# Batch 0's score steps in another order, and corner blocks cleared one group later

## The chip, the cores and the metric

One core of one Trainium2 chip. The metric is the device time of the whole program in microseconds (us), as the median of several runs. Each run has beside it the mean clock that TensorE was granted, as a share of full speed (1.0).

## The reference, cut to what matters

Eight batches of block-causal attention over 576 tokens (8 heads of 64, blocks of 64) are joined to 4608 tokens of 512 channels, which pass through an RMS norm and a gated feed-forward network (FFN).

```python
scores = scale * np.matmul(q, k.transpose(0, 1, 3, 2))      # 8 x 8 heads, 576 x 576
mask = block_i >= block_j                                   # blocks of 64
attn = np.exp(scores - max);  attn = attn / (sum + 1e-9)    # cut
x = (attn @ v), heads joined                                # 4608 x 512
rms = np.sqrt(np.mean(x * x, axis=-1, keepdims=True) + 1e-6)
xn = x / rms * rms_g
out = (silu(xn @ w_gate) * (xn @ w_val)) @ w_out            # 512 -> 1536 -> 512
```

## The kernel before

Heads go in pairs (b, t). `scores` makes a piece of S^T on TensorE, and ScalarE writes its exponential, unmasked, into `PT`. In each diagonal 128x128 tile one 64x64 corner lies outside the mask; VectorE sets it to zero (the "corner memset"). `values` multiplies by V: the P V product. `group` is one step of the FFN for 512 tokens (8 or 16 products on TensorE, `th` on ScalarE, then `gs` and `HT` on VectorE), and groups are laid between the attention steps so that TensorE always has something to do. The "scales" (`norm_scale`) multiply O^T, the output of P V, by the RMS factor; the result is `XT`, the input of the groups. The "ends" (`scores_ends`) are small 64x64 score blocks that are left over at the ends of the tokens.

```python
def clear(age=0):                                  # corner memsets, in VectorE's queue
    while corners and corners[0][0] <= gone - age:
        nc.vector.memset(corners.pop(0)[1], 0.0)

def scores_exp(pt, sp, step):
    nc.scalar.activation(out=pt[...], in_=sp[...], func=AF.Exp, scale=SCALE)
    for c, q0, w, o in parts:
        if c and q0 == c * P:                      # a diagonal tile: note its corner
            corners.append((gone, pt[BLK:P, :, lo + o:lo + o + BLK]))

def group(n=1):
    for _ in range(n):
        clear()                                    # every corner noted so far, AHEAD of gs and HT
        ...                                        # (cut) one FFN group: ffn_up or ffn_down
        gone += 1                                  # gone counts groups

def evacuate(outs, early=False):                   # behind a P V product
    ...                                            # O^T copy (VectorE if early, else ScalarE),
                                                   # then its square SQ on VectorE
```

The main sequence of batch 0 (cut; `FIRST` and `SECOND` are the two halves of the queries):

```python
scores(0, 0, "a"); transpose_pair(0, 1); scores(0, 0, "b"); fill(2)     # fill: zero matmuls
...                                                                     # (cut)
scores(0, 3, "a")
clear()                                             # all four pairs' corners at once
values(0, 0, FIRST, early=True)
values(0, 1, FIRST, early=True)
scores_ends(0)
...                                                 # (cut)
outs = values_mm(0, 0, SECOND, early=True)
...
group()
evacuate([head_product(0, ...)], True)
values(0, 2, SECOND, early=True)
values(0, 3, SECOND, early=True)
group()
```

The softmax here doesn't subtract the row's maximum and nothing guards it: scores larger than these inputs give would overflow.

## Time and profile before

| | before |
|---|---|
| time, median of 3 runs | 410.11 us (409.37 to 410.35) |
| span of the profiled run | 407.4 us |
| TensorE busy | 385.6 us, 95% |
| mean granted clock | 0.995 |

Two rows of the page that cut the span into 40 slices: TensorE's busy share in tenths, and the granted clock in tenths.

```profile
PE   7789799999999999999999999999999999999995
...
PEclk9989999999999999999999999999999999999999
```

The single 8 in the clock row is the third slice, 20 to 30 us: there lies the one stretch at half clock, 3.4 us long, and it costs the 0.005 by which the mean stays under 1. TensorE's longest waits, each as "engine, what it wanted to write, its line, the engine and tile that released it: us in total, how often, the longest".

```profile
PE fps L375 <- DVE w L367: 2.8, 6, 1.0
PE fps L451 <- DVE XT L420: 2.3, 9, 0.4
PE sps L237 <- DVE KT L206: 1.4, 3, 0.6
```

No P V product (L284) waits for the corner memset (L223).

### The profile page before, as it was taken

What the parts mean: (1) busy time and instruction counts of PE and PEld (TensorE: products, weight loads), DVE (VectorE), ACT (ScalarE), POOL (GpSimd) and SP (SyncE); (2) the same over time, 40 slices, a digit from 0 to 9 for tenths busy, and PEclk for the clock granted to TensorE, in tenths of its full rate; (3) what the DMA queues carried; (4) which work ended last, traced back from release to release, by engine and by line L of the source; (5) the groups of instructions that cost most, each with busy time, mean ns of one, the idle gap of its engine ahead of it and who ended that gap; (6) DMA issues with size and microseconds to landing.
All of it is one profiled execution on the core that took longest, in us unless ns stands there. A gap on an engine that the chain in (4) does not pass through costs nothing.

```text
span 407.4 us, 7780 instructions
## 1 busy us (share of the span) xinstructions
PE 385.6 (95%) x3048; PEld 183.7 (45%) x3087; DVE 251.3 (62%) x620; ACT 197.1 (48%) x283; POOL 129.0 (32%) x181
## 2 busy tenths in 40 slices
PE   7789799999999999999999999999999999999995
PEld 3468566444434444444444444444434434444442
DVE  5676876577777745376727764666457777555430
ACT  3825572466547753465546654565445213332321
POOL 8827773845028062670068004200110010100000
PEclk9989999999999999999999999999999999999999
DMA  8999999999919689999079915500020000010112
GB/s 108 171 202 186 188 140 154 174 137 172 111 53 127 69 78 129 139 139 116 2 108 138 139 19 77 79 0 2 28 78 2 0 27 26 15 38 27 51 52 78
DMA packets 139765, 36.43 MB, mean 89 GB/s; under 512 B 129233, under 2 KB 136913, under 8 KB 139729
## 3 DMA queue, kind: packets, MB, share of 16 engines
q0 software_dynamic: 108448, 26.75, 67.1%
q1 hardware_dynamic: 30752, 9.18, 15.4%
q8 instruction: 24, 0.39, 0.4%
q14 instruction: 13, 0.10, 0.1%
q10 hardware_dynamic: 528, 0.00, 0.1%
HBM read 38.80 MB, written 9.44 MB: 118 GB/s over the span
## 4 chain that ended last, share of the span: by engine, by line
PE 82%; DVE 10%; ACT 3%; issue 2%; DMA 1%; POOL 1%; DVEq 0%; ACTq 0%; POOLq 0%
PE fps L451 41%; PE fps L467 22%; PE sps L237 6%; PE sps L284 4%; PE fps L324 3%; DVE HT L459 2%; DVE XT L420 2%; DVE gs L457 2%; PE fps L284 2%; PE fps L427 1%; ACT th L455 1%; DMA nt<-in_k_dram 1%; PE fps L375 1%; ACT PT L245 1%; PE fps L199 1%
## 5 line engine op out<-in xcount | busy, mean ns | idle before, releaser
L451 PE MATMUL fps<-XT,WG 128*128 128x512 bf16 (+1 forms) x460 | 111.8, 358 | 3.6 <-DVE XT L420 2.3
L245 ACT ACTIVATE PT<-sps 128x1024 bf16<-128x1024 f32 (+1 forms) x96 | 93.8, 989 | 41.3 <-PE sps L237 40.8
L451 PE MATMUL fps<-XT,WV 128*128 128x512 bf16 (+1 forms) x479 | 110.9, 358 | 0.1
L457 DVE SCALAR_TENSOR_TENSOR gs<-th,fps 128x512 bf16<-128x512 f32 x108 | 74.2, 687 | 58.1 <-ACT th L455 56.9
L455 ACT ACTIVATE th<-fps 128x512 f32<-128x512 f32 x108 | 64.7, 599 | 70.7 <-PE fps L451 68.6
L467 PE MATMUL fps<-WO,HT 128*128 128x512 bf16 x416 | 96.4, 379 | 1.2 <-DVE HT L459 0.3
L459 DVE TENSOR_TENSOR HT<-gs,fps 128x512 bf16<-128x512 bf16 x108 | 74.3, 688 | 11.9 <-DVE gs L457 0.9
L451 PEld LDWEIGHTS <-WV 128*128 128x128 bf16 x480 | 46.9, 98 | 48.9 <-issue 3.2
L467 PEld LDWEIGHTS <-HT 128*128 128x128 bf16 x432 | 41.2, 98 | 51.9 <-issue 3.2
L451 PEld LDWEIGHTS <-WG 128*128 128x128 bf16 x480 | 42.3, 98 | 49.0 <-issue 13.3
L470 ACT ACTIVATE osb<-fps 128x512 f32<-128x512 f32 x36 | 21.5, 597 | 81.2 <-PE fps L467 74.2
L478 POOL DMA_DIRECT2D out_dram<-osb x22 | 12.7, 578 | 149.4 <-ACT osb L470 147.7
L123 POOL DMA_DIRECT2D VB<-in_v_dram x48 | 39.6, 845 | 17.3 <-PE sps L284 14.2
L420 DVE SCALAR_TENSOR_TENSOR XT<-OT,gscale,fps 128x64 bf16<-128x64 bf16 (+5 forms) x72 | 30.2, 476 | 21.9 <-PE fps L427 21.9
L237 PE MATMUL sps<-QT,KT 64*128 64x192 bf16 (+5 forms) x280 | 32.9, 310 | 2.6 <-DVE KT L206 1.4
L116 POOL DMA_DIRECT2D nt<-in_q_dram x30 | 26.1, 870 | 7.3 <-DMA VB<-in_v_dram 4.0
L116 POOL DMA_DIRECT2D nt<-in_k_dram x30 | 26.1, 871 | 5.8 <-PE fps L451 1.3
L223 DVE MEMSET PT<- 64x64 uint32 x96 | 9.3, 112 | 23.9 <-ACT PT L245 21.5
L284 PEld LDWEIGHTS <-VB 128*64 128x64 bf16 x344 | 14.7, 113 | 12.7 <-issue 4.4
L481 POOL DMA_DIRECT2D out_dram<-osb x12 | 6.6, 556 | 42.4 <-ACT osb L470 42.4
L237 PEld LDWEIGHTS <-KT 64*128 64x128 bf16 x280 | 9.1, 94 | 23.5 <-issue 18.8
L310 DVE TENSOR_TENSOR SQ<-OT 128x512 bf16<-128x512 bf16 (+1 forms) x44 | 15.7, 373 | 6.1 <-ACT OT L308 5.6
(69 smaller groups left out, 219.8 us busy)
## 6 DMA issues: line engine op xcount, KB each, us to landing
out_dram<-osb POOLq DMA_DIRECT2D x22, 256.0 KB, 2.4
VB<-in_v_dram POOLq DMA_DIRECT2D x32, 128.0 KB, 5.4
nt<-in_q_dram POOLq DMA_DIRECT2D x24, 128.0 KB, 5.5
nt<-in_k_dram POOLq DMA_DIRECT2D x24, 128.0 KB, 5.7
WG<-in_moe_w_gate_dram POOLq DMA_DIRECT2D x4, 384.0 KB, 9.7
WV<-in_moe_w_val_dram POOLq DMA_DIRECT2D x4, 384.0 KB, 10.9
WO<-in_moe_w_out_dram POOLq DMA_DIRECT2D x4, 384.0 KB, 7.7
out_dram<-osb POOLq DMA_DIRECT2D x12, 128.0 KB, 2.6
```

What stands on the lines that cost most here:

```text
L116: nc.gpsimd.dma_start(out=nt[0:rows, 0:512].rearrange("p (h d) -> p h d", h=H), in_=src[b, :, c * P:c * P + rows, :].rearrange("h p d -> p ...
L123: nc.gpsimd.dma_start(out=vb[r:r + n, cc, :].rearrange("p (h d) -> p h d", h=H), in_=v[b, :, tok:tok + n, :].rearrange("h p d -> p h d"))
L237: nc.tensor.matmul(sp[:, a, o:o + w], KT[b][r, t, c * P:(c + 1) * P], QT[b][r, t, q0:q0 + w], start=True, stop=True, skip_group_check=True)
L245: nc.scalar.activation(out=pt[:, :, lo:lo + width], in_=sp[:, :, 0:width], func=AF.Exp, scale=SCALE)
L284: nc.tensor.matmul(ov[a * D:(a + 1) * D, o:o + w], vb[:, c, h * D:(h + 1) * D], rhs, start=(i == 0), stop=(i == len(chunks) - 1), skip_gro ...
L420: nc.vector.scalar_tensor_tensor(out=XT[:, u, y0:y0 + hi - lo], in0=OT[b][:, u, j + lo:j + hi], scalar=gscale[:, u:u + 1], in1=src[:, lo:h ...
L451: nc.tensor.matmul(acc[:, i * w:(i + 1) * w], wt[c][:, p, r * P:(r + 1) * P], XT[:, p, x0:x0 + w], start=(p == 0), stop=(p == HP - 1), ski ...
L455: nc.scalar.activation(out=th, in_=g, func=AF.Tanh, scale=0.5)
L457: nc.vector.scalar_tensor_tensor(out=gs, in0=th, scalar=1.0, in1=g, op0=ALU.add, op1=ALU.mult)
L459: nc.vector.tensor_mul(out=HT[n][:, m:m + k, lo:lo + w], in0=gs.rearrange("p (k w) -> p k w", k=k), in1=u.rearrange("p (k w) -> p k w", k=k))
L467: nc.tensor.matmul(po, HT[n][:, m, i * P:(i + 1) * P], WO[:, m, :], start=(m == 0), stop=(m == NMC - 1))
L470: nc.scalar.mul(out=osb, in_=po, mul=0.5)
```

## The change

Its intent: keep ScalarE fed in batch 0 (its score steps come in another order, P V starts ahead of the last pair's scores), stop VectorE's queue from standing still in front of corner memsets whose exponential has not come yet (they are issued a group later), and put the scales of the second half of batch 0 behind a transpose and one more score step, so that TensorE has work while VectorE catches up. Since a corner can now be still uncleared when its pair's P V product is issued, that product first clears what is left of its own pair. The core of the diff:

```diff
+    def clear_pair(b, t):
+        for c in [c for c in corners if c[1] == (b, t)]:
+            corners.remove(c)
+            nc.vector.memset(c[2], 0.0)
     def values_mm(b, t, part=WHOLE, early=False):
         chunks, j0, width = part
+        clear_pair(b, t)
     def group(n=1):
         for _ in range(n):
-            clear()
+            clear(1)
 # batch 0 (more steps move in the same way; cut)
     scores(0, 3, "a")
-    clear()
-    values(0, 0, FIRST, early=True)
     values(0, 1, FIRST, early=True)        # values(0, 0, FIRST) now stands ahead of scores(0, 3, "a")
 # batch 1
+    transpose_pair(1, 2, on_act="qk")
+    scores(1, 1, 1)
     for u in range(HP):
         norm_scale("b", 0, 256, 320, u)
     mark(S)
-    transpose_pair(1, 2, on_act="k")
-    scores(1, 1, 1)
     group()
 # (cut) the ends of batch 1, scores_ends(1), move up by one group
-    clear()
     values(1, 3, early=True)
 # batch 2, last pair
-            values(2, HP - 1)
+            values(2, HP - 1, early=True)
+            evacuate([head_product(2, ps_f.tile([P, 512], FP32, name="fps"))], True)
```

## The prediction

> **What bounds the kernel now.** I read the page first, then the waits of the engines, then the stretches and the timeline of the first 105 us, because every edited line runs there.
>
> ```profile
> PE 385.6 (95%) x3048; PEld 183.7 (45%) x3087; DVE 251.3 (62%) x620; ACT 197.1 (48%) x283; POOL 129.0 (32%) x181
> PE 82%; DVE 10%; ACT 3%; issue 2%; DMA 1%; POOL 1%; DVEq 0%; ACTq 0%; POOLq 0%
> ```
>
> TensorE is busy 385.6 of 407.4 us and carries 82% of the chain that ended last. So only its idle time, 21.8 us, and any slow clock can be won, and any new idle time on it is lost one for one. The waits name what DVE stands still for:
>
> ```profile
> DVE PT L223 <- ACT PT L245: 21.5, 21, 4.9
> ```
>
> This is the corner memset (96 of them, 112 ns each) waiting in VectorE's queue for the exponential: 21.5 us. It looks like a prize, and "cleared a group later" goes for it. But nobody on TensorE is listed as waiting for these memsets, so in the kernel before it costs nothing.
>
> The stretches of the first 25 us show where TensorE is starved, and what follows:
>
> ```profile
> 18.00:21.30 3.30, 1.48 (x12) 0.73 (x9) 2.23 (x9) 1.81 (x2) 1.89 (x4) 1.00 1.31 203
> 21.30:24.70 3.40, 3.18 (x27) 1.89 (x28) 2.13 (x11) 1.02 (x1) 0.67 (x2) 0.50 1.32 203
> ```
>
> The first number after the length is TensorE's busy time, the third from the end the granted clock: 1.48 us busy in 3.30, then 3.4 us at half clock. Now three places in the timeline where P V products meet VectorE's queue:
>
> ```profile
> 27.85 0.19 DVE L223 MEMSET PT<- 64x64 uint32 x2
> 28.14 0.69 DVE L457 SCALAR_TENSOR_TENSOR gs<-th,fps 128x512 bf16<-128x512 f32 x1
> 28.93 0.69 DVE L459 TENSOR_TENSOR HT<-gs,fps 128x512 bf16<-128x512 bf16 x1
> 29.54 0.42 DVE L306 CAST OT<-fps 128x256 bf16<-128x256 f32 x1
> 29.99 0.29 DVE L310 TENSOR_TENSOR SQ<-OT 128x256 bf16<-128x256 bf16 x1
> ...
> 29.68 1.03 PE L451 MATMUL fps<-XT,WG 128*128 128x256 bf16 x8 [0.16 <-DVE HT L459]
> ```
> ```profile
> 62.47 0.26 DVE L223 MEMSET PT<- 64x64 uint32 x3
> 62.76 0.69 DVE L457 SCALAR_TENSOR_TENSOR gs<-th,fps 128x512 bf16<-128x512 f32 x1
> 62.88 0.79 PE L284 MATMUL fps<-PT,VB 128*64 128x512 bf16 x8
> 63.55 0.69 DVE L459 TENSOR_TENSOR HT<-gs,fps 128x512 bf16<-128x512 bf16 x1
> 63.61 1.05 PE L451 MATMUL fps<-XT,WG 128*128 128x256 bf16 x8
> ```
> ```profile
> 98.90 0.29 DVE L223 MEMSET PT<- 64x64 uint32 x3
> 100.35 0.79 PE L284 MATMUL sps<-PT,VB 128*64 128x512 bf16 x8
> 100.97 0.69 DVE L459 TENSOR_TENSOR HT<-gs,fps 128x512 bf16<-128x512 bf16 x1
> 101.57 0.68 DVE L306 CAST OT<-fps 128x512 bf16<-128x512 f32 x1
> 102.22 0.36 PE L237 MATMUL sps<-QT,KT 64*128 64x448 bf16 x2 [0.63 <-ACT OT L308]
> ```
>
> In each, the memset stands ahead of the gs and HT of the group, so the P V product just behind the group finds its corner already zero.
>
> **What the Trainium skill says.** "PSUM — Partial Sum Buffer", section Engine vs sequencer instructions: the queues of ScalarE and VectorE are strict FIFO. The trace agrees: DVE idles 21.5 us before memsets although later work is queued. "TensorE: Matmul & The Clock Gate", section Part 1: The HAM clock gate: TensorE falls to half clock after an idle window of about 3.4 us, and a free-running window decides. The trace agrees in size: 0.50 for the 3.4 us above. "Perfetto Trace Analysis", section Optimization Strategy: find the gaps of the bounding engine and the semaphore that ends each; I did that on the built order of both programs.
>
> **The change part by part.** The built order shows that all VectorE operations stay the same in number (two copies of Q or K go to ScalarE, one O^T of batch 2 and its head come to VectorE), TensorE gets 3 more filling matmuls (0.23 us each, as eight of that size take 1.83 us in the chain; all in idle time). What moves is what counts.
>
> (a) Batch 0 to its first gated group. P V of pair 0 no longer waits for the exponential of the last pair, so its O^T copy starts at about 14.95 instead of 16.40 us. But each pair's memsets now stand behind the square of the pair before, so DVE and TensorE take turns: 0.46 (copy) + 0.21 (square) + 0.2 (memsets) + 0.3 (last products) = 1.15 us per pair, instead of 0.67. The fourth square ends at about 19.0, where it ended at 19.1. Two fills put the transpose of the sums at about 19.75 (19.49 before). From there to the turned scales it is 4.4 us (19.49 to 23.89 before): about 24.15. Before, the scale products started at 24.66, not 23.9, because TensorE crawled at half clock; with the fills it should be warm. Then one score step is no longer between them and the first group. First group: about 25.9 instead of 26.5. Gain 0.55 us.
>
> (b) The second half of batch 0, pairs 2 and 3. Their last corner's memset now stands behind gs, HT and the head's copy and square. With the gain of (a), HT starts at 28.32, head copy 28.93, square 29.38, memset 29.6 to 29.7 us. Pair 2's product must stop before that corner from 28.3 to 29.75; pair 3's memset waits for pair 2's copy and square (30.0 + 0.46 + 0.21 + 0.1 = 30.8). The next group starts at about 31.0 instead of 29.68: loss 1.3 us net of (a), 1.85 us gross.
>
> (c) The scales of the second half behind a transpose and a score step. Before, from the end of the group at 43.09 to the end of the next at 49.3 us: 6.2 us. After, 1.0 us of transposes and scores fills the first wait, and VectorE has no Q copy there, but gs, HT (0.69 each) and four XT (0.48 start to start) still run one after another, and the group needs all four: about 5.9 us. Gain 0.3 us. The ends moved up save the 0.41 us wait at 53.53 but now wait themselves about 0.5 us for the Q copy behind gs and HT. Net of (c) 0.25 us gained.
>
> (d) P V of pair 2, batch 1: its two last corners are now cleared behind HT and the head (60.59 + 0.46 + 0.21 = 61.26, memset to 61.45), so its last chunks start at 61.42 instead of about 60.7, and the next group at 61.6 instead of 60.98. Loss 0.65 us.
>
> (e) P V of pair 3, batch 1. Counted from the start of the group before it (60.98): gs at +1.78, HT +2.57, memset +3.15, corner products +3.3 to +3.7; before, the next group started at +2.63. Loss 1.05 us.
>
> (f) P V of pair 3, batch 2: its memsets stand behind HT (100.97), pair 2's copy (101.57) and square (102.29): 102.6. The corner products start at about 102.75 and end at 103.2, then head 0.15, two score steps 0.4, next group at 103.8 instead of 102.75. The 0.63 us wait for ScalarE's copy is gone, and is in this difference. Loss 1.05 us.
>
> (g) Batches 3 to 7: a memset a group later still lands before its product, since at least one more group lies between. TensorE's remaining waits there are for w and XT, 0.2 to 0.4 us each, whose chains hold no memset. Zero.
>
> Sum: -0.55 + 1.85 - 0.25 + 0.65 + 1.05 + 1.05 = +3.8 us. To this comes the clock: (b) leaves TensorE idle for some 1.9 of 2.9 us, (c) for most of 3.3 us, and the turn-taking in (a) thins out 14 to 18 us. Half clock for 3.4 us costs up to 1.7 us of bound work. The stretch 41.80 to 45.20 had 1.86 us busy and kept its clock, so not every thin stretch falls. I take 0.5 of one such loss: +0.8 us. 410.1 + 3.8 + 0.8 = 414.7; I say 414.7.
>
> **The rivals.** First: the memset waits matter. 21.5 us of VectorE idle goes away, groups get through VectorE sooner, and TensorE with them. For it: the size, and VectorE is FIFO. Against: no TensorE wait names them, and in the batches that repeat TensorE is busy 98% (48.85 of 50 us from 200 to 250). It would give 405 to 408. Second: the warm clock is the prize. With the half clock gone and the order better for ScalarE, the first 50 us shorten by the idle there (2.3 us in 10 to 20, 1.7 in 20 to 30, 2.2 in 40 to 50 us), with no new stall: 407 to 409. Against: the built order puts memsets behind HT in (b), (d), (e), (f), and TensorE's wait is on exactly these. Third: the new gaps each trip the half clock: three times up to 1.7 us on top of 3.8, 417 to 419. For: the two lines of stretches above; against: 41.80 to 45.20.
>
> **Range and chances.** If the stalls are right and the clock stays, 413.9; if two of them trip it, about 417. If half of the stalls are hidden by something I missed, 412. So 411.3 to 417.8 should hold it 8 times in 10. Faster by over 2% needs under 401.9, more than all idle time of the first 105 us: 0.01. Slower by over 2% needs over 418.3, all clocks tripped: 0.06. The rest, 0.93, is within 2%.
>
> **What would show it.** Right: new lines among TensorE's waits, P V products waiting for the memset, some 1.4, 0.5, 0.7, 1.1 and 2.0 us long, near 28 to 31, 62, 65 and 104 us; the waits of memsets for the exponential nearly gone without gain; clock 1.00 from 21.3 to 24.7 us; stretches after 110 us unchanged but shifted by 4 us. Wrong: if P V never waits for a memset, (b) to (f) fall; if the first group comes later than 26.5 us, (a) falls, most likely by a half clock from 18 us on; if batches 3 to 7 shorten, the first rival is right.

## The result, and the profile after

| | before | after |
|---|---|---|
| time, median of 4 runs each, same chip | 410.21 us (409.37 to 410.35) | 421.33 us (419.27 to 421.49) |
| ratio, with its 95% interval | | 1.0264 (1.0229 to 1.0298): slower |
| span of the profiled run | 407.4 us | 419.7 us |
| mean granted clock, all runs | 0.995 (profiled) | 0.983 to 0.984 |

A ratio here is the mean time of one kernel's runs over that of the other's of the same rounds, so it is not quite the ratio of the medians that are quoted. The change costs 11 us; 4.6 were predicted (414.7 us, with 411.3 to 417.8 as the range).

The page of the changed kernel: TensorE's totals, its busy row and the clock row of 40 slices, and the shares of the chain that ended last.

```profile
PE 395.1 (94%) x3090; PEld 185.3 (44%) x3090; DVE 252.1 (60%) x620; ACT 197.4 (47%) x283; POOL 128.9 (31%) x181
...
PE   8787888999799999999999999999999999999995
...
PEclk9888999999899999999999999999999999999999
...
PE 81%; DVE 12%; ACT 4%; issue 1%; DVEq 0%; ACTq 0%
```

TensorE is busy 9.5 us *longer* than before, for the same work and 3 fills. Some 2 or 3 us of that are records that before's trace lacks (3048 matmuls against 3090; the later kernel k12_more_first, with all 3090 and at full clock while TensorE worked, shows 387.8). Most of the rest is a slower clock: the clock row has four 8s where it had one. VectorE's share of the chain rises from 10% to 12%. The waits of TensorE name the new cause (lines lie 5 or 6 further down in the changed kernel: P V is L290, and L228 is the memset in `clear_pair`):

```profile
PE fps L290 <- DVE PT L228: 8.0, 8, 2.2
PE fps L457 <- DVE XT L426: 3.1, 13, 0.4
```

The top line did not exist before: 8.0 us of P V products waiting for a corner memset, the longest 2.2 us. The 21.5 us for which VectorE stood in front of memsets are gone from VectorE's waits, as the change intended; nothing was won by it, for TensorE had never waited there.

Now the places. TensorE in the front of batch 0, where each pair's P V product stops before its corner (in brackets: the idle time before, and what ended it):

```profile
14.49 0.30 PE L290 MATMUL fps<-PT,VB 128*64 128x256 bf16 x2
15.68 0.30 PE L290 MATMUL fps<-PT,VB 128*64 128x192 bf16 x4 [0.89 <-DVE PT L228]
...
17.00 0.30 PE L290 MATMUL fps<-PT,VB 128*64 128x192 bf16 x4 [0.47 <-DVE PT L228]
...
18.31 0.43 PE L290 MATMUL fps<-PT,VB 128*64 128x192 bf16 x4 [0.36 <-DVE PT L228]
```

In the second half of batch 0, VectorE and TensorE of the changed kernel:

```profile
31.71 0.69 DVE L465 TENSOR_TENSOR HT<-gs,fps 128x512 bf16<-128x512 bf16 x1
32.32 0.41 DVE L312 CAST OT<-fps 128x256 bf16<-128x256 f32 x1
32.77 0.29 DVE L316 TENSOR_TENSOR SQ<-OT 128x256 bf16<-128x256 bf16 x1
...
33.11 0.11 DVE L228 MEMSET PT<- 64x64 uint32 x1
33.28 0.27 PE L290 MATMUL fps<-PT,VB 128*64 128x192 bf16 x2 [1.57 <-DVE PT L228]
```

Read the starts downward: HT of the group, the head's O^T copy, its square, and only then the one 0.11 us memset that the P V product has been waiting for. The product stood still for 1.57 us because of a memset of 0.11. The same in batch 2:

```profile
109.43 0.39 PE L290 MATMUL fps<-PT,VB 128*64 128x512 bf16 x2
...
111.84 0.26 DVE L228 MEMSET PT<- 64x64 uint32 x3
...
112.00 0.60 PE L290 MATMUL fps<-PT,VB 128*64 128x448 bf16 x6 [2.19 <-DVE PT L228]
...
113.33 1.89 PE L457 MATMUL fps<-XT,WG 128*128 128x512 bf16 x4
```

The product stops at 109.8, its memset comes at 111.84 behind HT, O^T and the square, and the group that follows takes 1.89 us for its first four products, which took 1.04 in every group of this shape around it. That is half clock. The stretches show it; they are cut at the boundaries of the clock's own windows as the drops give them, and the first number after the length is TensorE's busy time, the third from the end its clock.

```profile
13.95:17.36 3.41, 2.06 (x58) 1.29 (x52) 2.68 (x11) 2.58 (x3) 3.41 (x5) 1.00 1.52 137
17.36:20.78 3.42, 2.93 (x48) 1.55 (x48) 2.31 (x10) 1.63 (x3) 2.13 (x4) 0.50 1.31 200
20.78:24.19 3.41, 3.41 (x32) 0.84 (x24) 1.24 (x5) 1.58 (x2) 1.07 (x2) 0.50 1.31 204
31.02:34.43 3.41, 1.32 (x25) 0.92 (x25) 2.74 (x8) 0.00 (x0) 1.76 (x3) 1.00 1.22 205
34.43:37.84 3.41, 3.26 (x18) 2.27 (x18) 1.16 (x4) 0.60 (x1) 3.23 (x5) 0.50 1.43 192
109.52:112.94 3.42, 1.23 (x22) 0.67 (x18) 2.68 (x8) 0.00 (x0) 0.00 (x0) 1.00 0.55 108
112.94:116.35 3.41, 3.41 (x12) 1.04 (x8) 1.91 (x5) 2.12 (x3) 0.00 (x0) 0.50 0.76 82
```

While TensorE had work, four windows of 3.4 us ran at half clock: two in a row in the front, one behind the stall of batch 0, one behind the stall of batch 2. The drops begin at 17.36, 34.43 and 112.94 us, that is 17.1 and 95.6 us apart, 5 and 28 times 3.41: one grid that runs on whatever the kernel does. Each drop follows a window in which TensorE was busy 2.06, 1.32 or 1.23 of 3.41 us. This goes beyond what the prediction took from the Trainium skill, "TensorE: Matmul & The Clock Gate", section Part 1: The HAM clock gate, an idle window of about 3.4 us: TensorE was never idle for a whole window, the longest single gap was 2.19 us, and in the front 0.89 us.

The ledger of the two profiled runs, from the starts of the same FFN groups (before, after, difference), sums up where the 12.3 us between the two spans came from:

| up to this FFN group | before, us | after, us | difference | new since the line above |
|---|---|---|---|---|
| first group (a) | 26.43 | 29.16 | 2.73 | +2.73 |
| third group (b, and the half clock behind it) | 32.70 | 39.39 | 6.69 | +3.96 |
| the group after the scales and ends (c) | 54.31 | 61.16 | 6.85 | +0.16 |
| behind P V of pair 2, batch 1 (d) | 60.98 | 68.74 | 7.76 | +0.91 |
| behind P V of pair 3, batch 1 (e) | 63.61 | 72.68 | 9.07 | +1.31 |
| ahead of P V of pair 3, batch 2 | 98.47 | 107.55 | 9.08 | +0.01 |
| behind it (f, and the half clock) | 106.08 | 118.37 | 12.29 | +3.21 |
| end of the span (g) | 407.4 | 419.7 | 12.3 | 0 |

One part of the first line is not the change. The same eleven zero matmuls open both programs, and in these two runs they took (before, then changed):

```profile
1.19 4.03 PE L145 MATMUL fps<-zero 128*128 128x512 bf16 x11 [1.19 <-DVE zero L139]
1.19 4.88 PE L145 MATMUL fps<-zero 128*128 128x512 bf16 x11 [1.19 <-DVE zero L139]
```

The trace's first record of full clock begins at 4.2 us in the one and at 7.1 us in the other. In the fourteen profiled runs it begins between 4.2 and 7.1 us, and the first copy of Q starts between 5.66 and 6.73 us in the same order (k3_both, with the changed order, has 4.2 and 5.66): a matter of where the run meets the clock's grid, not of its program. The last copy of Q in the front, which starts at 13.17 us before and at 14.02 after, still has these 0.85 us between them. So 0.85 of the +2.73 is the luck of these two profiled runs, and the ledger's 12.3 us are 1.2 more than the 11.1 between the medians.

### The profile page after: what moved, and what is told of

It reads as the page before. It is cut to its first block, busy times and chain, and to the rows that moved or that the text cites. A ratio compares the mean times of both kernels' runs of the same rounds, so it can differ in the third digit from the quotient of the medians.

```text
span 419.7 us, 7824 instructions
## 1 busy us (share of the span) xinstructions
PE 395.1 (94%) x3090; PEld 185.3 (44%) x3090; DVE 252.1 (60%) x620; ACT 197.4 (47%) x283; POOL 128.9 (31%) x181
## 3 DMA queue, kind: packets, MB, share of 16 engines
q1 hardware_dynamic: 30752, 9.18, 14.1%
## 4 chain that ended last, share of the span: by engine, by line
PE 81%; DVE 12%; ACT 4%; issue 1%; DVEq 0%; ACTq 0%
PE fps L457 40%; PE fps L473 21%; PE sps L241 6%; PE sps L290 4%; PE fps L330 3%; DVE HT L465 3%; DVE gs L463 2%; DVE XT L426 2%; PE fps L290 2%; ACT th L461 2%; PE fps L145 2%; ACT PT L250 2%; PE fps L433 1%; PE fps L381 1%; DVE OT L312 1%
## 5 line engine op out<-in xcount | busy, mean ns | idle before, releaser
L457 PE MATMUL fps<-XT,WG 128*128 128x512 bf16 (+1 forms) x480 | 115.4, 363 | 3.1 <-DVE XT L426 3.1
L457 PE MATMUL fps<-XT,WV 128*128 128x512 bf16 (+1 forms) x480 | 112.2, 361 | 0.0
L473 PE MATMUL fps<-WO,HT 128*128 128x512 bf16 x432 | 97.6, 379 | 0.3 <-DVE HT L465 0.3
L476 ACT ACTIVATE osb<-fps 128x512 f32<-128x512 f32 x36 | 21.5, 597 | 81.2 <-PE fps L473 78.3
L290 PEld LDWEIGHTS <-VB 128*64 128x64 bf16 x344 | 14.6, 110 | 22.3 <-issue 10.7
L290 PE MATMUL fps<-PT,VB 128*64 128x256 bf16 (+5 forms) x120 | 12.5, 304 | 8.1 <-DVE PT L228 8.0
L241 PEld LDWEIGHTS <-KT 64*128 64x128 bf16 x280 | 9.0, 94 | 21.5 <-issue 16.7
```

Of the source, the lines that this page charges most:

```text
L241: nc.tensor.matmul(sp[:, a, o:o + w], KT[b][r, t, c * P:(c + 1) * P], QT[b][r, t, q0:q0 + w], start=True, stop=True, skip_group_check=True)
L290: nc.tensor.matmul(ov[a * D:(a + 1) * D, o:o + w], vb[:, c, h * D:(h + 1) * D], rhs, start=(i == 0), stop=(i == len(chunks) - 1), skip_gro ...
L457: nc.tensor.matmul(acc[:, i * w:(i + 1) * w], wt[c][:, p, r * P:(r + 1) * P], XT[:, p, x0:x0 + w], start=(p == 0), stop=(p == HP - 1), ski ...
L473: nc.tensor.matmul(po, HT[n][:, m, i * P:(i + 1) * P], WO[:, m, :], start=(m == 0), stop=(m == NMC - 1))
L476: nc.scalar.mul(out=osb, in_=po, mul=0.5)
```

## The experiments

The theory after the result: late clearing puts short memsets behind long work in VectorE's queue, TensorE stops for them at four places and takes turns with VectorE in the front; and the thinned stretches set off the half clock. The rivals: the new order of scores, scales and ends costs the time; lateness in program order costs by itself; the half clock has nothing to do with the stalls. Every run gave a correct result.

### Undoing the parts

k1_clear_now: the changed kernel with

```diff
-            clear(1)
+            clear()          # in group()
```

> The changed kernel, but each FFN group again clears every corner whose exponential has been issued, ahead of its own gs and HT, and not one group later. The turn-taking of VectorE and TensorE in the front of batch 0 stays. Theory: late clearing makes four stalls of TensorE at P V products (33 to 35, 68, 72 and 112 us; about 6.3 us together) and two of these trip the half clock (1.4 and 1.7 us). Then about 411.9 us (411 to 414), waits of P V for a corner memset only in the front (13 to 19 us), and two stretches of half clock fewer. Rival: the changed order of scores, scales and ends costs the time: over 418.

k2_front: the changed kernel with

```diff
+    clear()
     values(0, 0, FIRST, early=True)
 ...
+    clear()
     values(0, 2, FIRST, early=True)
```

> The changed kernel, but the corners of all pairs scored so far are cleared in one go ahead of the first P V product of batch 0 and again ahead of the third, so that VectorE and TensorE do not take turns there. The later clearing in the groups stays. Theory: the turn-taking thins TensorE's work at 14 to 18 us, and this is what drops the clock to half at 17 us. Then no half clock from 17 to 24 us, the first FFN group at about 26.5 to 27.5 instead of 29.2, and 418.6 to 419.5 us. Rival: the front is late for its start alone, and its clock falls whatever the waits: no change, about 421.

k3_both: both of these edits.

> The changed kernel with both of these undone: groups clear at once, and the front clears in one go. What is left of the change is its order. Theory: about 409.4 us (408.5 to 410.5), no wait of TensorE for a corner memset, mean clock 0.995 or more; the order alone is worth at most 1 us. Rival: order costs the time: over 416.

k4_late_only: the kernel *before*, with `clear_pair` in `values_mm` and `clear(1)` in `group`, and no step moved.

> The kernel before with its own order, and only the clearing changed: a group clears one group later, and each P V product clears what is left of its own pair's corners. Theory: clearing alone brings nearly all of the loss: about 419.6 us (416 to 420), waits of P V for a corner memset in batch 0 to 2 and a mean clock of about 0.985. Rival: the order is at fault and late clearing is hidden: 412 or less.

| | time, us | ratio to before (95%) | clocks of its runs |
|---|---|---|---|
| before, same chip, 7 runs | 410.34 (408.43 to 412.57) | | 0.982 to 0.999 |
| k1_clear_now | 411.60 (411.42 to 412.59) | 1.0042 (0.9991 to 1.0094) | 0.984 to 0.988 |
| k2_front | 416.37 (414.88 to 418.26) | 1.0156 (1.0097 to 1.0215) | 0.989 to 0.999 |
| k3_both | 408.54 (408.00 to 410.58) | 0.9978 (0.9912 to 1.0043) | 0.990 to 1.0 |
| k4_late_only | 418.92 (416.98 to 419.49) | 1.0208 (1.0151 to 1.0264) | 0.984 to 0.996 |

The rival "order" falls on both sides: with the clearing undone the new order is as fast as before (k3_both), and the old order with late clearing alone is 2.1% slower (k4_late_only). One word in `group` is worth nearly 10 us (k1_clear_now). Its waits of TensorE show what is left:

```profile
PE fps L457 <- DVE XT L426: 3.0, 13, 0.4
...
PE fps L290 <- DVE PT L228: 1.6, 3, 0.9
```

1.6 us in three waits, all in the front (here L228), instead of 8.0. One expectation missed: not two half-clock windows fewer but one, for a new one began at 50.67 us, behind a window in which TensorE was busy 1.71 of 3.41 us while TensorE waited for the scales. In k3_both, against what was expected, one wait of 0.9 us stayed, at the first P V product of the front, and its clocks were 0.990 to 1.0 and not all 0.995 or more.

k2_front came out better than expected, 416.4 instead of 418.6 to 419.5: its first group starts at 25.81 us and there is no half clock from 17 to 24 us, as the theory said, but in some of its runs the half clocks behind (b) and (f) stayed away as well (its run at clock 0.999 took 414.88 us). So a stall does not always drop the clock. k4_late_only shows such a case. It has the same waits of 1.58 and 0.67 us in batch 0, at 29.91 and 31.21, and its later drop at 108.22 us gives the grid of its run. Its windows around the stall:

```profile
26.30:29.71 3.41, 2.03 (x28) 1.54 (x26) 2.89 (x8) 1.16 (x2) 0.98 (x2) 1.00 1.31 203
29.71:33.13 3.42, 2.55 (x30) 2.05 (x29) 1.66 (x6) 0.60 (x1) 0.61 (x2) 1.00 1.27 205
33.13:36.54 3.41, 3.41 (x83) 2.70 (x82) 2.22 (x4) 0.60 (x1) 3.15 (x4) 1.00 1.21 203
```

The boundary at 29.71 falls into the stall and shares it out: busy 2.03 and 2.55 of 3.41, and the clock stays full. In the changed kernel nearly the whole stall lay in one window, busy 1.32.

A boundary is not the whole of it. In k8_late_b, told below, the stall of 1.57 us lay whole in one window, and the clock stayed full behind it:

```profile
27.45:30.86 3.41, 1.70 (x29) 1.12 (x27) 2.54 (x6) 0.25 (x1) 0.68 (x2) 1.00 1.32 207
```

I cut the first 122 us of all fourteen profiled runs in this way, each on its own grid. Of the windows at full clock in which TensorE was busy under 1.7 us, all 8 were followed by half clock; at 1.70 and 1.71 one of two; from 1.8 to 2.36 us, 7 of 38; above that, none of some 400. (Busy is the profile's number, so the limits are rough.) So a gap of 1.5 us or more can drop the clock; whether it does depends on how much work the rest of its window holds.

What this luck is worth, the kernel before shows with its 25 runs of the three sessions: 408.43 and 408.65 us at clock 0.999, 411.42 to 411.52 at 0.987, 412.57 at 0.982, 414.12 at 0.976. That is 5.7 us between the ends in one and the same kernel, so runs are compared by clock here, and a difference under 1 us between medians is rough. The mean clock is itself a rough guide: it leaves out the slow start told above, and it counts half clock after TensorE's last work, where it costs nothing (the profiled runs of k8_late_b and k12_more_first have 0.997 from that alone).

### Each stall by itself

Three kernels from k3_both, with the late clearing in only some groups:

```diff
-            clear()
+            clear(1 if gone < 2 else 0)              # k8_late_b: batch 0
+            clear(1 if 2 <= gone < 14 else 0)        # k9_late_de: batch 1
+            clear(1 if gone >= 14 else 0)            # k10_late_f: batch 2 and later
```

> The kernel with both clearings undone (k3_both, 408.5 us), with only the two groups beside the second half of batch 0 clearing late. Theory: the stall of part (b) alone, 2.5 us, and with luck of the clock 1 to 1.4 more: 411 to 412.5 us. By the size in the prediction it would be 410.4.

> The same kernel (k3_both), with only the groups of batch 1 clearing late, parts (d) and (e). Theory: 0.9 + 1.3 = 2.2 us with no half clock: 410.5 to 411 us. By the sizes in the prediction (0.65 + 1.05) it would be 410.2.

> The same kernel (k3_both), with only the groups from batch 2 on clearing late, part (f), and the zero of (g). Theory: 1.6 us and a half clock of up to 1.7: 410.1 to 411.8 us, nothing changed after 125 us. By the size in the prediction it would be 409.6. Rival for all three: the parts don't add, and the one that stays takes up what the others leave: each near 408.5, although all together cost 8.

| | time, us | ratio to before (95%) | over k3_both's 408.54 |
|---|---|---|---|
| before, 7 runs | 409.77 (409.01 to 411.49) | | |
| k8_late_b | 410.37 (410.22 to 410.61) | 1.0011 (0.9978 to 1.0043) | +1.8 |
| k9_late_de | 410.76 (410.31 to 410.96) | 1.0020 (0.9992 to 1.0048) | +2.2 |
| k10_late_f | 412.34 (411.57 to 412.91) | 1.0059 (1.0028 to 1.0089) | +3.8 |

1.8 + 2.2 + 3.8 = 7.8 us, and k2_front, which has all of them, is 416.37 - 408.54 = 7.8 us over k3_both (k3_both ran in the other session, where before was 0.6 us slower). So the parts add up, within the spread of k2_front's runs (414.88 to 418.26); all three lie well above 408.5, and the rival that they don't add is out. In k8_late_b the stall stands at full clock:

```profile
30.09 0.27 PE L290 MATMUL fps<-PT,VB 128*64 128x192 bf16 x2 [1.57 <-DVE PT L228]
...
31.40 0.27 PE L290 MATMUL fps<-PT,VB 128*64 128x192 bf16 x2 [0.68 <-DVE PT L228]
```

The same 1.57 and nearly the same second wait as in the changed kernel. First to second group took 31.63 - 25.97 = 5.66 us here and 28.46 - 25.16 = 3.30 in k3_both: part (b) is 2.36 us. k8_late_b missed its expected 411 to 412.5 from below; in its profiled run the clock did not fall behind the stall, and two of its other three runs had clock 1.0. k9_late_de came out as expected. k10_late_f missed from above:

```profile
103.44 0.60 PE L290 MATMUL fps<-PT,VB 128*64 128x448 bf16 x6 [2.19 <-DVE PT L228]
```

Its groups on either side of that product start 5.83 us apart, against 3.25 in k3_both: a stall of 2.6 us. I had expected 1.6, the loss measured against the kernel *before*, where O^T went by way of ScalarE and cost 0.63 us of its own. The profile also has the half clock behind it: the next stretch took 4.99 us instead of 3.55, another 1.4. 2.6 + 1.4 = 4.0.

### The same lateness in another queue

k7_clear_on_act: the changed kernel, but outside the front `clear_pair` uses ScalarE:

```diff
-            nc.vector.memset(c[2], 0.0)
+            nc.scalar.mul(c[2], c[2], 0.0)           # where part is not FIRST
```

> The changed kernel with the same lateness in program order, but what a P V product still has to clear of its own pair is cleared by ScalarE (a multiplication by zero) and not by VectorE; the front of batch 0 is left as in the changed kernel. Theory: the stalls come from the place of the memset in VectorE's queue, behind gs, HT, O^T and the square; ScalarE is idle there, so the stalls at 33, 68, 72 and 112 us vanish, and with them their half clocks. Then about 412 to 413.5 us. Rival: clearing late in program order costs by itself, whichever engine does it: 418 or more.

412.89 us (412.56 to 413.04), ratio 1.0072 (1.0045 to 1.0100), before 409.77. As late in program order as in the changed kernel, and 8.4 us faster than its 421.33. TensorE's waits for corners:

```profile
PE fps L293 <- DVE PT L231: 1.2, 2, 0.9
...
PE fps L293 <- ACT PT L229: 1.1, 1, 1.1
```

The first line is the front, which was left alone; at (b), (e) and (f) no wait is left, and at (d) 1.1 us, because there ScalarE had two exponentials ahead of the clearing (62.84 to 64.7 us): in ScalarE's queue, too, the place counts. One half clock stayed that the expectation did not have, from 49.01 us, behind a thin window at the scales as in k1_clear_now. In the second half of batch 0:

```profile
30.39 0.51 ACT L229 ACTIVATE PT<-PT 64x128 bf16<-64x128 bf16 x2
...
31.19 0.69 DVE L468 TENSOR_TENSOR HT<-gs,fps 128x512 bf16<-128x512 bf16 x1
...
31.93 1.03 PE L460 MATMUL fps<-XT,WG 128*128 128x256 bf16 x8 [0.16 <-DVE HT L468]
```

ScalarE clears both pairs' corners at 30.39 us, before VectorE has begun HT, and the next group starts 3.30 us after the one before it (28.63 to 31.93), as in k3_both. So it is the place in the clearing engine's queue that costs, not the lateness in program order.

### Stall and clock apart

k5_warm_gaps: the changed kernel with zero matmuls in the gaps of (b) and (f):

```diff
+        warm = {(0, 2, 256): (3, 6), (0, 3, 256): (3, 4), (2, 3, 0): (2, 9)}.get((b, t, j0))
         for i, (c, lo, w, o) in enumerate(chunks):
+            if warm and i == warm[0]:                # ahead of the chunk that needs the corner
+                f = ps_s.tile([P, 2, 512], FP32, name="sps")
+                for _ in range(warm[1]):
+                    nc.tensor.matmul(f[:, 0, :], zero[:, 0:P], zero, start=True, stop=True)
```

> The changed kernel with zero matmuls that nobody reads placed inside the three gaps of parts (b) and (f), where TensorE waits for VectorE's memset: 6 and 4 of them in the second half of batch 0, 9 in batch 2. They take no part in the result and fill idle time only, so the waits end when they did. Theory: the half clock after (b) and (f) comes from the idle time in these gaps; with the gaps filled the clock stays full from 31 to 125 us, and 1.4 + 1.7 us come back: about 418.2, mean clock 0.991. Rival: the clock falls for another reason, or the half clock costs nothing there: 421 as before.

418.41 us (417.66 to 419.05), ratio 1.0191 (1.0153 to 1.0230); the changed kernel had 1.0264. 2.9 us come back, as expected, and the clocks are 0.988 to 0.996 (the changed kernel: 0.983 to 0.984). In batch 2:

```profile
108.95 2.12 PE L291 MATMUL sps<-zero 128*128 128x512 bf16 x9
111.21 0.60 PE L295 MATMUL fps<-PT,VB 128*64 128x448 bf16 x6
...
112.38 1.04 PE L462 MATMUL fps<-XT,WG 128*128 128x512 bf16 x4
113.25 1.03 PE L462 MATMUL fps<-XT,WV 128*128 128x512 bf16 x4
```

The gap is now full of zeros, the corner products still start only when the memset allows (2.6 us after the start of the last ones ahead of them at 108.63, as in the changed kernel), but the next group's four products take 1.04 us, not 1.89. From the group ahead of the stall to the group behind the sums it is 115.93 - 106.75 = 9.18 us, and in the changed kernel 118.37 - 107.55 = 10.82: the half clock behind (f) costs 1.64 us, and the gap sets it off. At (b) this run is less clean: no half clock follows the filled gaps, but one fell just *ahead* of them, from 28 to 32 us, behind another thin stretch, so that from the first to the third group both kernels took 10.23 us. So that the total came out as expected is partly luck: of the 2.4 us between the two profiled runs 1.64 are (f), and the other 0.8 were there before (b), as this run started earlier. The size of the clock's part at (b) comes from k8_late_b instead: 34.67 - 25.97 = 8.70 us at full clock, against 10.23, so 1.53.

k11_front_fills: k1_clear_now with fills in the turn-taking of the front:

```diff
         for i, (c, lo, w, o) in enumerate(chunks):
+            if part is FIRST and i == 1:
+                fill((4, 2, 1, 0)[t])
```

> The changed kernel with the groups clearing at once (k1_clear_now, 411.6 us), and zero matmuls in the gaps of the front where TensorE takes turns with VectorE: 4, 2 and 1 in the P V products of pairs 0, 1 and 2. Theory: of the 3 us between k1_clear_now and k3_both the turn-taking itself is about 1 us and the half clock that it sets off the other 2: 409.3 to 410 us and no half clock from 16 to 23 us. Rival: the turn-taking alone costs the 3 us: 411.5 with a full clock, or the clock falls in spite of the fills.

409.30 us (408.88 to 410.77), ratio 0.9976 (0.9937 to 1.0015). It keeps the clock full where k1_clear_now fell at 16.5 us; the stretch around the turn-taking, with TensorE busy all through:

```profile
13.50:17.00 3.50, 3.50 (x56) 1.68 (x50) 2.81 (x11) 2.44 (x3) 3.50 (x6) 1.00 1.83 149
```

The three kernels split the front: k1_clear_now 411.60, k11_front_fills 409.30, k3_both 408.54. By the medians turn-taking is 0.8 us and the half clock 2.3. The traces split it more cleanly, from the last copy of Q in the front to the first group: 11.99 us in k3_both, 13.76 in k11_front_fills, 15.63 in k1_clear_now. So turn-taking is 1.8 us and the half clock that it sets off 1.9. k3_both then loses 0.8 us of its lead, because it now reaches the transposes of batch 1 before their loads have landed:

```profile
33.75 0.47 PE L199 MATMUL fps<-ident,nt 64*64 64x64 bf16 x18 [0.35 <-DMA nt<-in_q_dram]
34.42 0.47 PE L199 MATMUL fps<-ident,nt 64*64 64x64 bf16 x18 [0.20 <-DMA nt<-in_k_dram]
```

and k1_clear_now has the second half clock at 50.67 us, about 1.0 us, which k11_front_fills has not. In the four profiled runs with unfilled turn-taking (the changed kernel, k1_clear_now, k5_warm_gaps, k7_clear_on_act) the clock fell in the front, between 14.9 and 18.3 us; in those of the changed order without it, or with it filled, it did not fall before 25 us.

### A version that beats both

k12_more_first takes k3_both and puts one more transpose and score step ahead of the scales; k13_ends_later only moves the ends:

```diff
 # k12_more_first
     scores(1, 1, 1)
+    transpose_pair(1, 3, on_act="qk")
+    scores(1, 1, 2)
     for u in range(HP):
         norm_scale("b", 0, 256, 320, u)
     mark(S)
     group()
     fetch(2, 3)
-    transpose_pair(1, 3, on_act="k")
-    scores(1, 1, 2)
     scores_ends(1)
 # k13_ends_later
     scores(1, 1, 2)
-    scores_ends(1)
     group()
     fetch(2, 3)
+    scores_ends(1)
     scores(1, 2, 0)
```

> A try at a better kernel from k3_both: one more transpose and score step ahead of the scales of the second half of batch 0, so that TensorE has work while VectorE does gs, HT and the four XT, with both copies of the transpose on ScalarE; the ends of batch 1 behind the group. Part (c) says that such work is free there: 0.5 to 1.5 us less than k3_both, 407 to 408. Rival: the scales come later by what they stand behind, and the group waits for them all the same: 408.5.

> k3_both with one thing moved: the ends' scores of batch 1 go one group later, as TensorE waited 0.77 us there for VectorE's copy of Q behind gs and HT. Theory: the 0.77 us come back, 407.7 to 408. Rival: the wait only moves on: 408.5.

(In k12_more_first the ends stay behind the scales' group, where k3_both has them.)

| | time, us (5 rounds) | ratio to before (95%) |
|---|---|---|
| before, 11 runs | 410.05 (409.65 to 414.12) | |
| k12_more_first | 406.82 (406.63 to 407.54) | 0.9911 (0.9878 to 0.9944) |
| k13_ends_later | 408.30 (407.19 to 409.42) | 0.9947 (0.9914 to 0.9981) |

k12_more_first beats the kernel before by 0.9% (its runs, 406.63 to 407.54, lie all below those of k3_both, which ran in another session) and the changed kernel by 14.5 us; 407 to 408 was expected. The stretch from 42 to 55 us in k3_both:

```profile
42.00:55.00 13.00, 10.29 (x159) 6.97 (x157) 9.33 (x24) 8.17 (x12) 8.88 (x12) 1.00 1.71 180
```

and in k12_more_first:

```profile
42.00:55.00 13.00, 11.30 (x172) 7.64 (x169) 9.63 (x25) 9.36 (x14) 8.77 (x11) 1.00 1.76 185
```

TensorE is busy 1.0 us more of the same 13 us: the transposes and scores lie in what were waits for gs, HT and the copy of Q. k13_ends_later, expected at 407.7 to 408, gains little: at clock 1.0 its runs took 407.69 and 407.85, those of k3_both 408.00 and 408.22, so about 0.3 of the 0.77 us. The wait at the ends is gone, and one of 0.38 us for the ends' exponential has come at 54.29: most of it moved on.

## Why the prediction was wrong

| step | predicted, us | measured, us | from |
|---|---|---|---|
| (a) first group, at full clock | -0.55 | +0.50 | k11_front_fills (below) |
| clock in the front | 0 | +1.38 | below |
| start of the profiled run, not the change | 0 | +0.85 | 14.02 - 13.17 |
| (b) pairs 2, 3 of batch 0 | +1.85 | +2.43 | 3.96 in the ledger less 1.53 of clock |
| (c) scales and ends | -0.25 | +0.16 | ledger |
| (d), (e) batch 1 | +1.70 | +2.22 | ledger; k9_late_de +2.2 |
| (f) batch 2 | +1.05 | +1.57 | 3.21 in the ledger less 1.64 of clock |
| (g) batches 3 to 7 | 0 | 0 | ledger |
| clock behind (b) and (f) | +0.8 | +3.17 | 1.53 + 1.64 |
| sum | +4.6 | +12.3 | spans 419.7 - 407.4 |

**Right:** the mechanism of (b), (d), (e), (f): short memsets behind HT, O^T and squares, with P V waiting for them. The waits appear at the named places (1.4, 0.5, 0.7, 1.1 and 2.0 us were predicted; 1.57, 0.67, 0.73, 1.12 and 2.19 came), k1_clear_now removes them, k7_clear_on_act shows that the queue is the cause, and k8 to k10 show that they add. That the 21.5 us of VectorE's idle time were worth nothing, and (g), were right too.

**Wrong, the step that failed:** the clock. The prediction says of (a) "with the fills it should be warm", and of the rest "I take 0.5 of one such loss: +0.8 us". In the front the turn-taking that it had worked out itself thinned TensorE's work ahead of the fills, the clock fell at 17.36 us in the profiled run, and the fills then ran at half speed. From the last copy of Q in the front to the first group it is 13.26 us before, 15.14 in the changed kernel, and 13.76 in k11_front_fills, which takes the same turns at full clock. So of the +2.73 of the ledger 0.85 is the late start, 1.38 the half clock, and 0.50 is (a) itself. Behind (b) and (f) the changed kernel's profile has a full loss each time, not half of one in all: 3.17 instead of 0.8. The clock thus makes 1.4 + 2.4 = 3.8 of the 7.7 us by which the sum is off. The prediction had named the sign itself: a first group later than 26.5 us, "most likely by a half clock from 18 us on"; it came at 29.16.

The third rival, new gaps that each trip the clock, was the one to believe, though its 417 to 419 was still too low; it was set aside on the strength of one stretch that kept its clock. That stretch had 1.86 us busy, where 7 windows of 38 fall; the stalls of (b) and (f) leave 1.0 to 1.7 in a window unless a boundary cuts them. And the cut is luck: k4_late_only and the changed kernel have the same stall in batch 0 and opposite clocks behind it.

**Right in kind, off in size:** the turns in the front, 1.15 us per pair predicted and 1.32 measured (O^T copies at 15.43, 16.75, 18.06 and 19.39 us in k11_front_fills); and the stalls, 4.6 predicted and 6.2 measured. At (b) the prediction has the next group 5.1 us after the first one; it was 5.78, and 5.66 in k8_late_b at full clock. HT and the memset came 0.1 to 0.2 later than worked out, and from pair 3's memset to the next group it took 0.40 us (31.23 to 31.63 in k8_late_b) where 0.2 was allowed. At (f) a reading was off as well: the line at 102.75 has three of that group's four products, so in the kernel before this group began near 102.5, and the loss was counted some 0.2 us too small. (c) gained nothing here; in k12_more_first, with twice as much work ahead of the scales, the idea works.

**Left open:** what decides among windows of 1.8 to 2.36 us busy, where the front's window lies (2.06). The mean clocks of all runs of the changed kernel and of k1_clear_now are alike (0.983 to 0.988), but where the clock fell is seen only in the profiled runs. And undoing the front's turn-taking gained 3.1 us on k3_both's side (411.60 - 408.54) and 5.0 on the changed kernel's (421.33 - 416.37). 0.8 of the difference is k3_both's wait for the loads of batch 1; I take the rest for the luck of clock and start, but that was not shown.

## What to carry to other kernels

An instruction that another engine waits for must stand in its queue ahead of the long work, even if its own engine then stands idle for it: idle time of an engine that is not the bound is free, and a 0.11 us memset behind 1.4 us of other work (HT, O^T and a square) is not. Before moving something later, ask who waits for it and what stands in front of it in the new place. And count the clock with each new gap of TensorE: a stall of 1.6 to 2.2 us can cost another 1.5 us behind it, so take that loss in full unless the window around it stays well filled, look at runs by their granted clock, and put idle matmuls into gaps that can't be avoided.

## What the Trainium skill lacked or had wrong

- "TensorE: Matmul & The Clock Gate", sections Part 1: The HAM clock gate and HAM oscillation — how this bites in real kernels: the page says that the clock follows how busy TensorE has been, but the rule that it gives is about idle gaps of more than about 3.4 us, with no busy share. Here the clock fell to 0.50 behind windows whose longest gap was 0.89, 1.57 or 2.19 us. What went with it was the busy time of the whole window: under 1.7 of 3.41 us, 8 of 8 fell, at 1.70 and 1.71 one of two, from 1.8 to 2.36 us 7 of 38, above that none of some 400. The window's length and that it runs free agree with the traces (drops 17.1 and 95.6 us apart in one run).
- The same page doesn't say that a boundary inside a stall can save the clock: the same stall left 1.32 us busy in one window and dropped it, and 2.03 and 2.55 in two and did not.
- The same page tells of the window's phase only at the start of a kernel; it doesn't say what it does to a comparison: 25 runs of one kernel went from 408.43 us at clock 0.999 to 414.12 us at 0.976, 1.4%.
